# A gated-attention and convolution kernel: g_norm by rows, batch 0 by one cast queue, the norm spread in 32-row pairs, copies and order set anew

## The chip, the cores and the metric

The kernel runs on one core of a Trainium2 chip. The core has TensorE (PE, matrix products into PSUM), VectorE (DVE), ScalarE (ACT), GpSimd (POOL) and SyncE (SP); each runs its own instructions in order, and they wait for one another by semaphores. Loads and stores are issued from the queues of SP, ACT and POOL and run on 16 DMA engines that all queues share; a load issued by POOL can change fp32 to bf16 on its way. The metric is the device time of one execution in microseconds, median of the runs.

## The reference

Eight batches, eight heads, a sequence of 576, a head dimension of 64; the joined model dimension is 512, the inner one 1024.

```python
kv = np.einsum('bhsd,bhse->bhde', k, v)
out = np.einsum('bhsd,bhde->bhse', q, kv)
rms = np.sqrt(np.mean(out * out, axis=-1, keepdims=True) + 1e-06)
x = out / rms * g_norm                       # then (B, S, H * D)
h = np.maximum(x @ w_in, 0.0)
conv_out = sum(conv_w[k] * hp[:, k:k + S, :] for k in range(3))   # hp: h padded by one row at both ends
gate = 1.0 / (1.0 + np.exp(-conv_out))
y = (h * gate) @ w_out
```

The first four lines are the attention without softmax and its norm per head; the rest is a gated network with a convolution over the sequence in each of the 1024 channels.

## The kernel before, in words

Everything is kept transposed: channels on the 128 partitions, the 576 positions of a batch along the free dimension. Two heads (64 + 64 channels) make one of four head pairs t of a batch b. The program is a list of small operations, each a Python function, and the string `ORDER` says in which order they are issued; each engine then runs its own in that order. A token such as `hm.0.3@1` names the operation, its arguments and, behind the @, the buffer that its result takes: rings `a` (three double-bank PSUM buffers) and `b` (two PSUM banks) and several rings in SBUF. A buffer's next user waits for the last reader of the one before.

The operations: `pre` sets constants and issues the first loads; `Lq`, `Lk`, `Lv`, `Li`, `Lo` load q, k, v, w_in and w_out by POOL with a change to bf16; `ca` casts batch 0's first two head pairs, which SP loads as fp32 (L301). `kv` (L313) forms k transposed times v for n head pairs; `kvc` copies the 64x64 blocks into the block-diagonal `kvbd`. `qt`/`qt0` transpose q on PE in 24 or 12 small products, `qc`/`qc0` copy the result to SBUF. `ot` (L377) is the attention product o; `sq` squares it on ACT, `oc` copies it to SBUF.

The norm has two forms. Batch 0 goes head pair by head pair: `on` sums the squares with a block matrix of ones, `nl` takes the reciprocal root, `mu0` multiplies o, g_norm and the root. All other batches go by groups (`NORM`): `ss` sums the squares into 32 partitions for each head pair, `ln` takes the reciprocal root for all in one ACT instruction, `sl` splits it into three bf16 parts on DVE, `sp` (L449) spreads it back to 128 channels by products with the 0/1 matrix `spread`, and `mu` multiplies.

Then `hm` (L466) is one of eight 128-channel blocks of x @ w_in, eight products of 288 columns; `re` the relu copy. `ta` multiplies by the two outer convolution weights, scaled by the middle one (which `ct` transposes and `pc` prepares), `aa` and `ab` add, `sg` is the sigmoid, `mg` the gate product. `om` (L523) is one of nine 128-position blocks of the product with w_out for a pair p of batches, 8 products of 512 columns, in two halves of four for p 0 and 3; `ea` copies the result to SBUF and `st` stores it. `pl`, `ps`, `pn` build `sel`, `spread` and the masks `na`, `nb`.

Of the kernel before, what the change touches and what calls it, by code (L numbers as in the profile page):

```python
# [51 lines left out]
FP32 = mybir.dt.float32  # L52
BF16 = mybir.dt.bfloat16
AX = mybir.ActivationFunctionType
AL = mybir.AluOpType
PSUM = bass.MemoryType.PSUM

NORM = {0: [1], 1: [2, 3], 2: [4, 5], 3: [6, 7]}
CONV = {0: (0, 1), 1: (1, 1), 2: (2, 2), 3: (4, 2), 4: (6, 1), 5: (7, 1)}
# [3 lines left out]
pre@0,0,0,1 ca.q.0 qt0.0@0 qc0.0@0 ca.k.0 ca.v.0 kv.0.0.1@0 kvc.0.0.1.0 kvc.0.0.1.1 ot.0.0@1 sq.0.0@0 on.0@2  # L63
ca.v.1 ca.k.1 ca.q.1 qt0.1@0 kv.0.1.1@1 kvc.0.1.1.1 nl.0@0 Lk.1.0@1 qc0.1 kvc.0.1.1.0 qt0.2@2 ot.0.1@0
kv.0.2.1@0 qc0.2@1 sq.0.1@1 kv.0.3.1@1 on.1@2 kvc.0.2.1.0 mu0.0@0 kvc.0.2.1.1 nl.1@1 ot.0.2@1 kvc.0.3.1.0
Lv.1.0@1 sq.0.2@2 ct@0 on.2@2 nl.2@2 kvc.0.3.1.1 mu0.1 Lq.1.0@1 Li.0 pc Lk.1.2 qt0.3@0 mu0.2 qc0.3 ot.0.3@2
sq.0.3@3 kv.1.0.2@1 on.3@0 kvc.1.0.2.0 pl Lq.1.2 qt.1.0@1 nl.3@3 mu0.3 hm.0.0@0 re.0.0@0 qc.1.0@2 kvc.1.0.2.1
hm.0.1@2 ot.1.0@1 re.0.1 Lv.1.2 qt.1.1@0 Li.1 ta.0.0@0 hm.0.2@2 ps ta.0.1 qc.1.1@3 sq.1.0@4 oc.1.0@4 re.0.2 pn
kv.1.2.2@0 ta.0.2@1 kvc.1.2.2.0 ot.1.1@1 kvc.1.2.2.1 hm.0.3@2 sq.1.1@5 oc.1.1@5 re.0.3 ot.1.2@0 aa.0.0 sq.1.2@6
ot.1.3@1 sq.1.3@7 hm.0.7@2 oc.1.3@6 ss.1@1 oc.1.2@7 ln.0@0 ab.0.0 re.0.7 Lv.2.0@0 Lk.2.0@0 ta.0.3 aa.0.1 sl.0@0  # L70
hm.0.5@1 re.0.5 hm.0.4@0 ab.0.1 re.0.4 sp.1.1@2 sp.1.0@1 sg.0.0 kv.2.0.4@0 sp.1.2@0 mu.1.0 mu.1.1 sp.1.3@1
sg.0.3 hm.0.6@2 mu.1.2 mu.1.3 Lq.2.0@0 qt.2.1@0 sg.0.1 mg.0.0 kvc.2.0.4.0 kvc.2.0.4.1 re.0.6 hm.1.7@1 sg.0.2
re.1.7 Lv.3.0@1 qc.2.1@4 ot.2.3@2 sq.2.3@0 Lk.3.0@1 hm.1.5@0 ot.2.2@1 oc.2.3@0 re.1.5 sq.2.2@1 ta.0.4@0 ta.0.5
oc.2.2@1 aa.0.2 ab.0.2 hm.1.6@2 sg.0.5 sg.0.4 qt.2.0@0 qc.2.0@0 hm.1.2@1 Lq.3.0@1 re.1.6 re.1.2 hm.1.3@0
ot.2.0@2 mg.0.1 kv.3.0.4@1 re.1.3 mg.0.2 ta.0.6@1 oc.2.0@2 sq.2.0@2 ot.2.1@1 kvc.3.0.4.0 oc.2.1@3 sq.2.1@3
hm.1.4@0 ta.0.7 Lo.0 aa.0.3 kvc.3.0.4.1 ta.1.6@0 Lo.1 qt.3.1@2 ab.0.3 sg.0.6 qc.3.1@1 qt.3.0@1 qc.3.0@2 ot.3.3@2
re.1.4 om.0.1.0@0 sg.0.7 mg.0.3 sq.3.3@4 ot.3.1@0 sq.3.1@5 oc.3.1@4 ta.1.4@1 ot.3.0@1 om.0.2.0@1 sq.3.0@6
om.0.2.4 ea.0.2@0 ta.1.7 ot.3.2@0 sq.3.2@7 oc.3.2@5 om.0.1.4 ss.2@1 ea.0.1@1 ta.1.5 ss.3 ln.1@0 oc.3.0@7 aa.1.3
ab.1.3 aa.1.2 Lq.5.0@0 qt.5.0@0 qc.5.0@3 oc.3.3@6 om.0.3.0@0 om.0.3.4 sl.1@1 ea.0.3@2 om.0.0.0@1 ab.1.2 hm.1.1@0
re.1.1 sg.1.5 sg.1.7 sp.2.0@1 sp.3.1@2 mu.2.0@1 om.0.0.4 sg.1.4 mu.3.1 Lv.5.0@0 Lk.5.0@0 sp.2.2@0 mu.2.2  # L80
sp.2.3@1 ea.0.0@3 kv.5.0.4@0 sp.2.1@2 hm.1.0@0 re.1.0 mu.2.3 sp.3.2@1 Lq.6.0@1 mu.2.1 sg.1.6 hm.2.0@2 sp.3.3@0
mu.3.2 Lk.4.0@1 re.2.0@1 kvc.5.0.4.0 mg.1.2 mu.3.3 Lk.6.0@0 ta.1.2@1 kvc.5.0.4.1 hm.2.5@1 re.2.5 sp.3.0@2
Lv.4.0@1 mu.3.0 ta.1.3 aa.1.1 mg.1.3 hm.2.7@0 ab.1.1 re.2.7 ot.5.0@1 sq.5.0@0 ta.1.0@0 hm.2.1@2 oc.5.0@2 re.2.1
hm.3.1@0 re.3.1 sg.1.3 ta.1.1 hm.3.0@1 re.3.0 qt.5.1@2 sg.1.2 qc.5.1@4 hm.2.6@0 re.2.6 aa.1.0 ot.5.3@1 oc.5.3@4
sq.5.3@1 kv.4.0.4@1 ot.5.1@2 oc.5.1@1 sq.5.1@2 hm.3.7@0 kvc.4.0.4.0 mg.1.1 re.3.7 hm.2.3@1 re.2.3 Lq.4.0@0
ab.1.0 ta.2.0@1 hm.3.3@2 sg.1.0 ta.2.1 hm.3.2@0 aa.2.0 sg.1.1 ab.2.0 re.3.2 mg.1.0 re.3.3 kvc.4.0.4.1 hm.2.2@1
# [500 lines left out]
```

## Time and profile before

| what | value |
|---|---|
| runs | 194.63, 195.0, 196.04 us, median 195.0 |
| profiled execution | span 192.5 us from the first to the last instruction |
| PE busy | 171.1 us (89%), 1753 products |
| DVE busy | 148.8 us (77%), 279 instructions |
| ACT busy | 153.5 us (80%), 246 instructions |
| POOL busy | 25.7 us, 39 instructions |
| granted TensorE clock | 1.000 |
| loads by POOL | 15.37 MB as landed, 52.7% of the 16 DMA engines over the span |

Some groups of instructions of the page (mean of one by form): sq 673 ns, oc 662, re 658, ea 605, sigmoid 775 for 576 and 1251 for 1152 elements, table load 1283 (eight of them), all on ACT; mu 810, qc 754, aa, ab and mg 757 for 1152 and 1355 for 2304 elements, a tap product 373 or 540, the two casts of batch 0's k and v 615 to 634, on DVE.

How to read it: busy time is the union of an engine's instructions; those queued behind one another overlap a little, so that the sum of their durations is larger. Idle time of an engine that is not the last to be ready costs nothing. The chain of waits goes back from the last instruction to whatever released each step.

### The profile page before, as it was taken

The numbers are of one execution on the slowest core, as the hardware profiler recorded it, in microseconds if no ns is written. First come the engines' busy times: TensorE is split into PE (matmuls) and PEld (weight loads), VectorE is DVE, ScalarE is ACT, GpSimd is POOL, SyncE is SP. The second block draws the span as 40 slices with busy tenths as digits, with TensorE's granted clock in tenths as the row PEclk, the third lists the DMA queues.
The fourth block names the chain that finished last, engine by engine and source line by source line (L and its number), as shares of the span: only waits on it lengthen the run. The fifth ranks groups of instructions, "written<-read, shape, count | busy, mean of one in ns | idle before, by whom it ended". The sixth has DMA issues, their size and how long they took to land.

```text
span 192.5 us, 4249 instructions
## 1 busy us (share of the span) xinstructions
PE 171.1 (89%) x1753; PEld 106.9 (56%) x1753; DVE 148.8 (77%) x279; ACT 153.5 (80%) x246; POOL 25.7 (13%) x39
## 2 busy tenths in 40 slices
PE   0047799899999999999999999999999999999992
PEld 0024366566745777764658776654477485554440
DVE  3133839897988999999989999999989895977100
ACT  2047648999999899999999999999996869478431
POOL 7435303400430111240000000000000000000000
PEclk9999999999999999999999999999999999999999
DMA  4999999999999997999950000441040010170874
GB/s 135 207 236 204 203 204 203 204 204 206 186 203 204 182 130 118 137 120 188 208 185 5 0 3 0 165 167 54 0 163 3 0 54 3 54 272 0 327 266 170
DMA packets 26517, 26.84 MB, mean 139 GB/s; under 512 B 1388, under 2 KB 21892, under 8 KB 26500
## 3 DMA queue, kind: packets, MB, share of 16 engines
q0 software_dynamic: 19872, 15.37, 52.7%
q1 hardware_dynamic: 6432, 11.21, 16.3%
q8 instruction: 13, 0.21, 0.4%
q10 hardware_dynamic: 196, 0.01, 0.1%
q14 instruction: 4, 0.03, 0.1%
HBM read 32.52 MB, written 9.44 MB: 218 GB/s over the span
## 4 chain that ended last, share of the span: by engine, by line
PE 70%; DVE 11%; ACT 8%; DMA 6%; issue 2%; SPq 1%; ACTq 0%
PE h_ps L471 28%; PE om_ps L528 27%; DMA stg<-in_q_dram 6%; PE qt_ps L343 4%; PE sp_ps L454 4%; PE kv_ps L319 3%; ACT sq L388 2%; PE o_ps L374 2%; DVE taps L493 2%; DVE taps L500 2%; DVE taps L506 2%; DVE taps L494 1%; ACT o L393 1%; ACT h L479 1%; DVE h L518 1%
## 5 line engine op out<-in xcount | busy, mean ns | idle before, releaser
L471 PE MATMUL h_ps<-xT,w_in_sb 128*128 128x288 bf16 x512 | 70.1, 290 | 0.7 <-ACT o L393 0.3
L528 PE MATMUL om_ps<-w_out_sb,h 128*128 128x512 bf16 x288 | 66.7, 379 | 0.1
L471 PEld LDWEIGHTS <-w_in_sb 128*128 128x128 bf16 x512 | 50.0, 99 | 17.1 <-issue 1.5
L479 ACT ACTIVATE h<-h_ps 128x576 bf16<-128x576 f32 x64 | 40.6, 658 | 9.3 <-PE h_ps L471 9.0
L528 PEld LDWEIGHTS <-h 128*128 128x128 bf16 x288 | 27.8, 98 | 30.2 <-issue 0.7
L512 ACT ACTIVATE taps<-taps,cw 128x576 bf16<-128x576 bf16 (+1 forms) x48 | 42.9, 933 | 1.0 <-DVE taps L506 0.9
L534 ACT ACTIVATE row<-om_ps 128x512 f32<-128x512 f32 x36 | 21.8, 605 | 10.7 <-PE om_ps L528 10.4
L518 DVE TENSOR_TENSOR h<-h,taps 128x1152 bf16<-128x1152 bf16 (+1 forms) x24 | 22.7, 953 | 5.7 <-ACT taps L512 5.7
L500 DVE TENSOR_TENSOR taps<-taps 128x1152 bf16<-128x1152 bf16 (+1 forms) x24 | 23.0, 958 | 0.5
L343 PE MATMUL qt_ps<-ident,q_sb 96*64 96x96 bf16 x384 | 12.6, 221 | 12.0 <-ACT q_sb L305 11.9
L506 DVE TENSOR_TENSOR taps<-taps,h 128x1152 bf16<-128x1152 bf16 (+1 forms) x24 | 22.9, 956 | 0.5
L493 DVE TENSOR_SCALAR taps<-h,cw 128x576 bf16<-128x576 bf16 (+1 forms) x48 | 20.8, 434 | 2.5 <-ACT h L479 2.5
L460 DVE SCALAR_TENSOR_TENSOR xT<-o,g_sb,sp_ps 128x576 bf16<-128x576 f32 x28 | 21.2, 810 | 1.8 <-PE sp_ps L454 1.8
L494 DVE TENSOR_SCALAR taps<-h,cw 128x576 bf16<-128x576 bf16 (+1 forms) x48 | 20.3, 423 | 0.0
L343 PEld LDWEIGHTS <-q_sb 96*64 96x64 bf16 x384 | 10.4, 120 | 15.9 <-ACT q_sb L305 12.4
L388 ACT ACTIVATE sq<-o_ps 128x576 bf16<-128x576 f32 x28 | 18.1, 673 | 0.1
L393 ACT ACTIVATE o<-o_ps 128x576 f32<-128x576 f32 x28 | 17.8, 662 | 0.0
L374 PE MATMUL o_ps<-qT,kvbd 128*128 128x512 bf16 x32 | 12.7, 409 | 0.0
L196 ACT ACT_TABLE_LOAD x8 | 10.3, 1283 | 2.8 <-issue 2.6
L368 DVE COPY qT<-qt_ps 128x1152 bf16<-128x1152 bf16 x14 | 10.4, 754 | 1.7 <-PE qt_ps L343 1.4
L454 PE MATMUL sp_ps<-wparts,spread 128*128 128x288 bf16 x56 | 9.9, 287 | 1.0 <-ACT h L479 0.7
L276 POOL DMA_DIRECT2D q_sb<-in_q_dram x8 | 6.0, 748 | 34.5 <-PE qt_ps L343 29.0
(66 smaller groups left out, 100.2 us busy)
## 6 DMA issues: line engine op xcount, KB each, us to landing
out_dram<-row SPq DMA_DIRECT2D x36, 256.0 KB, 2.6
v_sb<-in_v_dram POOLq DMA_DIRECT2D x6, 576.0 KB, 9.4
k_sb<-in_k_dram POOLq DMA_DIRECT2D x6, 576.0 KB, 11.3
q_sb<-in_q_dram POOLq DMA_DIRECT2D x6, 576.0 KB, 9.1
w_in_sb<-in_moe_w_in_dram POOLq DMA_DIRECT2D x2, 512.0 KB, 12.8
w_out_sb<-in_moe_w_out_dram POOLq DMA_DIRECT2D x2, 512.0 KB, 15.6
stg<-in_k_dram SPq DMA_DIRECT2D x2, 288.0 KB, 6.2
stg<-in_v_dram SPq DMA_DIRECT2D x2, 288.0 KB, 7.0
```

What stands on the lines that cost most here:

```text
L343: nc.tensor.transpose(ps[i * D:(i + 1) * D, r * PS:(r + 1) * PS], qkv["q", b][:, 2 * t + i, r * D:(r + 1) * D], ident[:PS, :PS])
L388: nc.scalar.activation(by_r(s), natural(o), AX.Square)
L471: nc.tensor.matmul(ps[:, e, :HS], w_in_sb[:, t, f * P:(f + 1) * P], x[:, t, e * HS:(e + 1) * HS], start=(t == 0), stop=(t == NT - 1))
L479: nc.scalar.activation(T["h", b // 2][:, f, b % 2, :].rearrange("p (e n) -> p e n", e=2), T["hm", b, f][:, :, :HS], AX.Relu)
L493: nc.vector.tensor_scalar_mul(tap[:, 0, f % 2, :n, 8:8 + S], h[:, f], cw[:, f:f + 1])
L494: nc.vector.tensor_scalar_mul(tap[:, 1, f % 2, :n, :S], h[:, f], cw[:, 2 * NF + f:2 * NF + f + 1])
L500: nc.vector.tensor_add(tap[:, 1, :, :n, :S], tap[:, 0, :, :n, 7:7 + S], tap[:, 1, :, :n, 1:1 + S])
L506: nc.vector.tensor_add(y, y, h[:, 2 * j:2 * j + 2])
L512: nc.scalar.activation(y, y, AX.Sigmoid, scale=cw[:, NF + f:NF + f + 1])
L518: nc.vector.tensor_mul(h, h, T["tap", c, j][:, 1, :, :n, :S])
L528: nc.tensor.matmul(T["om", p, m], h[:, f, m * P:(m + 1) * P], w_out_sb[:, f, :], start=(f == 0), stop=(f == NF - 1))
L534: nc.scalar.activation(T["os", p, m], T["om", p, m], AX.Copy)
```

## The change

It has five parts.

1. g_norm is loaded twice as a 256-byte row, side by side in a 25th row of `cw_rows`, and the transpose `ct` of the convolution weights brings it to the partitions too; `g_sb` is a column of that result (`cw`, copied by the new `pg`). The scaled weights get a tile of their own, `cwn`.
2. SP loads only k and v of batch 0's first head pair as fp32. The other ten pieces of batch 0 come by POOL with a change to bf16, two of them issued ahead of `affine_select`, which makes the identity.
3. `sp` uses for each head pair only the 32 rows that hold its part, at its place in the array, and does two head pairs in one operation, their products in turn; `spread` shrinks from 2048 to 512 elements, and a pair takes two `a` buffers at once.
4. Every copy out of PSUM (`kvc`, `qc0`, `qc`, `oc`, `re`, `ea`) can run on DVE or ACT by a digit behind a colon in the order. In the new order DVE takes 9 of 28 oc, 7 of 64 re, 5 of 36 ea, 7 of 24 kvc and 1 of 4 qc0; ACT takes 4 of 14 qc and 17 kvc. An oc on DVE waits for the square of the same o on ACT. `pl` fills `sel` on POOL. A `+n` in the order would add filling products; no token has one.
5. The order is new throughout: batches 4 and 5 are loaded ahead of w_out, and batch 4 is attended ahead of batch 5.

```diff
-pre@0,0,0,1 ca.q.0 qt0.0@0 qc0.0@0 ca.k.0 ca.v.0 kv.0.0.1@0 kvc.0.0.1.0 kvc.0.0.1.1 ot.0.0@1 sq.0.0@0 on.0@2
...
+pre@0,0,0 ca.k.0 ps pi ca.v.0 kv.0.0.1@0 ct@1 Lv.1.0@1 qt0.0.0@0 Lq.1.0@1 Lk.1.0@1 pg kv.0.1.1@1 qt0.0.2@1 Li.0
+Lq.1.2 qt0.0.1@2 pc kvc.0.0.1.0@0 qc0.0.0:1@0 kvc.0.1.1.0:1 kvc.0.0.1.1:1 al.x0@0 qc0.0.2:1@1 al.h1@0 kvc.0.1.1.1
+al.h0@1 ot.0.0@0 al.x1@1 sq.0.0@0 on.0.0@1 nl.0.0@0 kv.0.2.1@0 qc0.0.1:1 kvc.0.2.1.0 kvc.0.2.1.1 ot.0.2@1 sq.0.2@1
...
+ss.3 qc.4.1@3 hm.1.4@2 hm.1.2@1 ln.1@0 ta.1.1 oc.3.0@7 qt.4.0@0 re.1.4 sl.1@0 aa.1.0 re.1.2 Lq.5.0@1 sp.3.0@2,1
+mu.3.0 mu.3.1 qc.4.0:1@4 Lv.5.0@1 Lk.5.0@1 sp.2.1@0,2 mu.2.2 mu.2.3 Lo.0 kv.4.0.4@0 Lo.1 sg.0.4 kvc.4.0.4.0@0
+kvc.4.0.4.1 sp.2.0@1,0 mu.2.1 mu.2.0 sg.0.5 ot.4.1@2 sq.4.1@0 qt.5.0@0 oc.4.1@7 ot.4.2@1 sq.4.2@1 mg.0.2 hm.2.2@2
...
+mg.5.0 st.3.0 re.7.6:1 ta.5.6@0 ta.5.7 sg.5.4 ea.3.3@5 om.2.2.0@0 sg.5.5 aa.5.3 om.2.5.0@1 st.2.0 ab.5.3 ea.2.2@3
+om.3.7.0@0 mg.5.2 ea.2.5@6 st.2.2 sg.5.6 st.3.3 sg.5.7 st.2.6 om.2.1.0@1 st.2.5 mg.5.3 ea.2.1@7 om.3.7.4 ea.3.7@1
+om.3.5.0@1 om.3.8.0@0 om.3.5.4 ea.3.5@3 om.3.8.4 ea.3.8@5 om.3.6.0@1 om.3.4.0@0 om.3.6.4 st.3.7 st.2.1 st.3.5
+om.3.4.4 ea.3.6:1@2 st.3.8 st.3.2 st.3.1 st.3.6 ea.3.4@6 st.3.4
...
-        for t in range(2):
-            for x in "kvq":
-                nc.sync.dma_start(out=T["stg"][:, "kvq".index(x), t], in_=heads(x, 0, 2 * t, 2))
+        for i, x in enumerate("kv"):
+            nc.sync.dma_start(out=T["stg"][:, i], in_=heads(x, 0, 0, 2))
...
-            nc.scalar.dma_start(out=g_sb[i * D:(i + 1) * D, :], in_=g_norm.unsqueeze(1))
+            nc.scalar.dma_start(out=cw_rows[NC:, i * D:(i + 1) * D], in_=g_norm.unsqueeze(0))
         act_table("rs")
+        nc.vector.memset(fill, 1.0)
...
+        for n, (x, t) in enumerate([(x, t) for t in range(NT) for x in "kvq" if t or x == "q"]):
+            if n == 2:
+                nc.gpsimd.affine_select(
+                    out=ident, in_=ident, compare_op=AL.not_equal, fill=1.0,
+                    base=0, pattern=[[-1, P]], channel_multiplier=1)
+            nc.gpsimd.dma_start(out=qkv[x, 0][:, 2 * t:2 * t + 2, :], in_=heads(x, 0, 2 * t, 2))
...
+    def after(ins, other):
+        if ins.engine != other.engine:
+            tc.add_manual_dep(
+                ins, other.name,
+                mybir.DependencyInfo(mybir.DependencyClass.Sync, mybir.DependencyReason.DATA), reason="bank")
+
+    def copy(to, fr, on_act):
+        if on_act:
             nc.scalar.activation(to, fr, AX.Copy)
         else:
             nc.vector.tensor_copy(to, fr)
...
-        nc.scalar.activation(by_r(s), natural(T["ot", b, t][:, :S]), AX.Copy)
+        copy(by_r(s), natural(T["ot", b, t][:, :S]), pick[0] == 0)
+        after(last(), T["sqi", b, t])
...
-    def sp(b, t):
+    def sp(b, u):
         g = NG[b]
         bi = NORM[g].index(b)
-        ps = T["sp", b, t] = ring("a", [P, 2, 512], FP32, name="sp_ps")
+        for t in (2 * u, 2 * u + 1):
+            T["sp", b, t] = ring("a", [P, 2, 512], FP32, name="sp_ps")
         for e in range(2):
-            nc.tensor.matmul(
-                ps[:, e, :HS], spread[:, t * 4 + 2 * bi + e, :, :].rearrange("p i d -> p (i d)"), T["w", g],
-                start=True, stop=True)
+            for t in (2 * u, 2 * u + 1):
+                rows = slice(t * 32, (t + 1) * 32)
+                nc.tensor.matmul(
+                    T["sp", b, t][:, e, :HS], spread[rows, 2 * bi + e, :, :].rearrange("p i d -> p (i d)"),
+                    T["w", g][rows], start=True, stop=True, tile_position=(t * 32, 0))
...
+        if pick[0] == 0:
+            nc.scalar.activation(to, fr, AX.Relu)
+        else:
+            nc.vector.tensor_scalar(to, fr, 0.0, None, op0=AL.max)
```

## The prediction

> **What bounds the kernel now.** I read the page's busy times and slices first, then the table of busy times by stretch, then the chain of waits in order of time, then the timeline of the start. The stretches (columns: stretch, its length, then PE, weight loads, DVE, ACT and POOL busy with instruction counts, clock, DMA share, GB/s):
>
> ```profile
> 5.00:10.00 5.00, 0.00 (x0) 0.00 (x0) 0.71 (x1) 0.59 (x1) 2.40 (x4) 1.00 0.97 215
> 10.00:15.00 5.00, 2.31 (x28) 1.16 (x28) 1.60 (x4) 1.99 (x4) 2.18 (x3) 1.00 1.24 228
> ...
> 30.00:40.00 10.00, 8.75 (x136) 5.81 (x132) 9.15 (x22) 9.51 (x18) 3.80 (x5) 1.00 1.32 204
> 40.00:50.00 10.00, 9.53 (x134) 6.67 (x130) 8.76 (x16) 9.95 (x19) 2.06 (x3) 1.00 1.28 205
> 50.00:60.00 10.00, 9.45 (x171) 5.90 (x170) 9.08 (x21) 9.84 (x19) 1.79 (x3) 1.00 1.28 195
> 60.00:70.00 10.00, 10.00 (x110) 6.72 (x109) 8.77 (x14) 9.37 (x15) 1.54 (x2) 1.00 0.98 159
> 70.00:80.00 10.00, 9.98 (x141) 7.62 (x139) 9.87 (x21) 9.60 (x19) 1.78 (x2) 1.00 0.90 130
> ```
>
> Four stages. Nothing runs on PE until 10.3 us (loads). From 10 to 26 us batch 0 goes through one serial chain per head pair. From 26 to 60 us ACT is full (29.3 of 30 us) and the loads run at 204 GB/s. From 60 us on PE is full to 188.8 us; then a copy and a store end the span. Busy PE overstates its work, so I priced each product from pieces of the chain where PE runs without a gap:
>
> ```profile
> 63.60 0.49 PE sp_ps L454 x4
> 64.09 0.86 PE om_ps L528 x4
> ...
> 66.68 0.98 PE h_ps L471 x8
> ...
> 74.67 0.63 PE qt_ps L343 x24
> 75.30 1.09 PE h_ps L471 x8
> ```
>
> That is 0.1225 us for a spread or h product, 0.216 for an om product, 0.63 for 24 transposes, 0.88 for 48 kv products. Over the program: h 62.7, om 62.2, transposes 10.1, kv 7.0, o and on 8.6, spread 6.9, ss 2.4: 160 us. PE ends at 188.8, so it lost 28.8 us: 20.4 before its first h product (25.9 us less 5.5 us of work issued by then), about 6 between 26 and 60 us, about 2 later. The profiled execution's span is 192.5 us; the median run is 195.0, so 2.5 us lie around the span, and I add them at the end.
>
> **The spread (sp).** Before, 56 products of 128 rows one after another: 56 x 0.1225 = 6.86 us, all on a full PE or just before it becomes full. After, the same 56 work on 32 rows each, in pairs on different rows into different PSUM tiles. If the two of a pair overlap wholly, 28 x 0.1225 = 3.43 us: 3.43 saved. The trace has no products side by side in rows. It has them side by side in columns, the sums of squares:
>
> ```profile
> 35.40 0.43 PE L427 MATMUL ss_ps<-sq,sel 128*32 128x288 bf16 x8
> ```
>
> Eight of 0.286 us each within 0.43 us; in a row they would need 0.98. So bounds are 0 (no overlap) and 3.43; I take overlap, by this nearest row. Against it: the 8 h products behind a block of transposes take 1.09 us, and 0.98 behind a spread, so 0.11 goes where the array changes its shape. The 14 blocks of pairs could pay that once each, 1.5 us, or nothing; I take 0.7. Net -2.7 us.
>
> The Trainium skill, page "TensorE: Matmul & The Clock Gate", section on packing small matmuls, reports 3.07 times for four 32-row products; as an estimate from that, a pair would run some 1.5 times as fast and save 2.4 us. The Trainium skill, "TensorEngine Tiling (Array Packing)", section Tiling Modes, says that a change of tiling mode drains the array, which speaks against pairs strewn between full products; the 0.11 us above agrees in sign.
>
> **The start.** Before, batch 0's first two head pairs come as fp32 by SP, and ACT and DVE cast them; the first transposes wait for q:
>
> ```profile
> 9.41 0.84 ACT L305 ACTIVATE q_sb<-stg 96x768 bf16<-96x768 f32 x1 [5.50 <-DMA stg<-in_q_dram]
> 10.31 0.50 PEld L343 LDWEIGHTS <-q_sb 96*64 96x64 bf16 x12 [10.31 <-ACT q_sb L305]
> ...
> 25.68 0.82 DVE L413 SCALAR_TENSOR_TENSOR xT<-o_ps,g_sb,o 128x576 bf16<-128x576 f32 x1 [1.60 <-ACT o L404]
> ```
>
> k and v of the first pair landed at 4.0 and 5.0 us; the six SP loads alternated with the POOL loads from then on (one of each per 1.8 us). After, SP brings only those two, and ten cast loads of 0.63 to 0.75 us issue time follow on POOL. Between loads of POOL alone, landings 0.72 us apart for 144 KB are 204 GB/s. From about 5 to 6 us for q of pair 0 the seventh load, q of pair 2, lands at about 10.5 (bounds: 9.5, and 12.6, where the third POOL load landed before). PE's new order has the transposes of pairs 2 and 1 ahead of the first o product, so that starts at about 11.2 us, where it was 11.9. Four rounds o, square, on, root, multiply follow, 13.8 us before (11.9 to 25.7). In these the first root stood on ACT behind q's second cast, which waited for its load until 14.57 and ended at 15.3, 1.4 us after the product for it; that wait goes, of which I count 0.8, since the kvc copies now on ACT fall in its place. The last multiply then starts at 11.2 + 13.0 = 24.2 instead of 25.7: -1.5 us, bounds -3 and +1 (q of pair 2 at 12.6). w_in's first half had 885 KB of batch 0 and 885 of batch 1 ahead of it on POOL and landed at 22.8; it now has 1,475 and 885, but four SP loads fewer: not later. ACT's two casts (1.7 us) and two of DVE's (1.2) go, beside waits.
>
> g_norm came as two loads of 64 pieces (landing 5.3 and 6.7 us after issue) and is now two rows transposed with conv_w. ct moves ahead of the first transposes and waits for these rows, at the latest 8.7 us; queued behind it on PE are all of batch 0's products, but the first o product waits past 10 us anyway: nothing, or up to 1.6 us if the loads came early. The two extra issues ahead of affine_select (1.4 us) delay ident to 2.5 us, before the first cast at 4.1. The fill tile costs one memset (0.27 us, row of kvbd's) at the start: the order has no token that asks for fills.
>
> **Copies.** From ACT go 9 oc (0.662), 7 re (0.658), 5 ea (0.605), 1 qc0 (0.648) and 2 casts (0.842): 15.9 us; it gets 4 qc of 1152 elements, at most the sigmoid's 1.25 each, 5.0. ACT falls from 153.5 to about 142.6. DVE gets the 22 copies at ACT's price, 14.2 us (bounds 0.5 and 0.81 each, by its casts from SBUF and its multiply L460), and loses 4 qc (3.0), 2 casts (1.2), about 1.0 of spread, 0.6 of sel (now POOL), 0.5 of small ones: from 148.8 to about 157. Summed durations are 8% above busy time because queued instructions overlap by some 0.09 us; if that overlap were complete, 149. I take 153. So DVE becomes the fuller engine. Adding both orders' instructions by these rows, less the overlap: up to its 35th us of PE work the old order asks 41 us of ACT and 37 of DVE, the new one 40.5 and 43. Where ACT was late in the stretch 26 to 60, DVE is late now: I book 0, with bounds -2.4 (ACT's relief counts fully; the loads allow no more, since k of batch 5 has 11.4 MB ahead on POOL, 56 us at 204 GB/s from a start at 5 to 9, and is due after 37 us of PE work: PE has lost at least 24 us by then, against 26.4 before) and +5 (DVE as below). A new wait: an oc on DVE must follow ACT's square of the same tile; behind it on DVE stand conv taps that ACT's sigmoids wait for. At up to a square's 0.67 us each, nine are 0 to 6 us of idle DVE, inside the bound of +5. pl's nine memsets now stand on POOL ahead of batch 2's loads, whose predecessors are still in flight: 0. The tail: after the last h product 24 om products more than before cover the chain ta, aa, ab, sigmoid, mg (about 11 us, covered by 12.1): 0, or +1.
>
> **Sum.** 192.5 - 2.7 - 1.5 = 188.3 span, + 2.5 = **190.8 us**.
>
> **Rivals.**
> *DVE becomes the bound (slower).* By 25 us DVE has done about 7 us; its last mg has 9 half om blocks (7.8), a copy and store (3.7) behind it. Span = 25 + 146/u + 11.5, u its use until then. u = 0.96 gives the forecast's 188.6, 0.92 195.2, so 197.7 us; each per cent is 1.6 us. For it: 90% between 30 and 60 us. Against: 97% from 70 to 130. It decides below 0.94. Chance 0.22, times 194 to 200.
> *Slots.* A pair holds two of three PSUM slots until its multiplies. At batches 2 and 3 the order sets sp.3.0, sp.2.1, kv.4, sp.2.0, ot.4.1, qt.5.0 in a row with no om block between: an add of 0.7 and five multiplies of 0.78 are 4.6 us on DVE before qt.5.0 gets its slot, beside 1.9 us of PE work: 2.7 lost, 193.5. For it: there the old order has om blocks, and w_out now comes later. Against: the same stretch is bound by DVE anyway. Chance 0.11.
> *The pairs bring nothing.* Draining into and out of each of 14 blocks at 0.11 costs 3.1 and eats the 3.43; or the rows don't overlap, which is the case where the change doesn't do what it says: 193.2 to 194. Chance 0.10. The first would be the rule of the Trainium skill, "TensorEngine Tiling (Array Packing)", section Tiling Modes.
> *More.* ACT's relief counts fully and DVE keeps up: 190.8 - 2.4 - some of the start: 187. Chance 0.15.
>
> **Numbers.** The forecast's own case has 0.42, between 188.8 and 193. About 1% (1.95 us) is what a measurement tells from no change. Faster by over 1% (below 193.05): forecast, "more" and 0.01 of the slots: 0.58. Within: 0.08 of slots, 0.10 of pairs, 0.04 of DVE's: 0.22. Slower (above 196.95): 0.18 of DVE's, and 0.02 where slots and DVE add up: 0.20. Range 185.5 to 197.5: below lies the far end of "more", above the worse half of DVE's.
>
> **What would show it.** Pairs: 8 spread products within 0.5 us, an h block behind them at 0.98 to 1.1. Start: first o product near 11.2, first h product near 24.5. Copies: DVE over 95% from 30 to 130 us, ACT below 95%. It would be wrong if PE shows waits for DVE between 60 and 130 us, or if q of pair 2 lands after 12.6.

## The result, and the profile after

The changed kernel takes 198.23 us (median of 13 runs, 196.1 to 199.69) and the kernel before, beside it, 194.63 (193.74 to 196.04): 1.0145 times as long, 95% interval 1.0116 to 1.0174. The ratio leaves disturbed runs out, so it is a little below that of the medians. The prediction was 190.8 us with a range of 185.5 to 197.5: the kernel is some 1.5% slower where faster was forecast, and outside the range. The profiled execution took 196.1 us, with a span of 194.3, and is the shortest of the 13.

The table of busy times by stretch, of the changed kernel (columns as before: stretch, length, PE, weight loads, DVE, ACT, POOL, clock, DMA share, GB/s):

```profile
5.00:10.00 5.00, 1.71 (x37) 1.55 (x37) 3.13 (x17) 0.87 (x2) 5.00 (x9) 1.00 1.30 195
10.00:15.00 5.00, 2.86 (x40) 1.67 (x40) 0.80 (x1) 3.07 (x7) 4.66 (x14) 1.00 1.31 199
30.00:40.00 10.00, 7.38 (x124) 4.89 (x122) 9.89 (x18) 9.65 (x16) 1.78 (x3) 1.00 1.32 204
40.00:50.00 10.00, 9.42 (x177) 6.75 (x172) 9.18 (x19) 8.81 (x16) 3.69 (x5) 1.00 1.20 177
50.00:60.00 10.00, 7.71 (x147) 4.62 (x145) 9.32 (x18) 9.88 (x15) 2.53 (x4) 1.00 1.31 203
60.00:70.00 10.00, 9.61 (x153) 6.50 (x146) 8.78 (x16) 8.80 (x17) 4.54 (x6) 0.83 1.28 205
70.00:80.00 10.00, 9.97 (x79) 5.46 (x78) 9.06 (x19) 9.67 (x16) 0.11 (x1) 1.00 1.32 204
```

The first two rows are better than before, and three are worse. PE works from 6.2 us on, where it had nothing until 10.3. But from 30 to 40 us it is busy for 7.38 us instead of 8.75, from 50 to 60 for 7.71 instead of 9.45, and from 60 to 70 its clock is 0.83 on average where it was 1.00. Busy time does not tell how much work is done at half a clock, so I priced every product as the prediction did and subtracted: "lost" is the time so far less the work of the products started so far, so it holds waits and slow clock together. The prices are 0.1225 us for one product of h or spread, 0.216 of om, 0.63 for 24 transposes, 0.88 for 48 of kv, 0.24 for an o or on, and 0.043 for one of ss. The last two rows are experiments told below.

| lost by PE, us | by 26 us | by 50 | by 65 |
|---|---|---|---|
| before | 20.8 | 25.8 | 26.7 |
| changed | 18.4 | 23.7 | 29.0 |
| before with the new start alone | 17.7 | 21.9 | 22.2 |
| before with start, rows and pairs | 18.4 | 22.6 | 23.1 |

At 26 us the changed kernel leads by 2.4 us, at 50 by 2.1, at 65 it is 2.3 behind. From 70 us on PE is nearly full in both. So the change wins at the start and loses 5.3 us between 50 and 65, where the kernel before loses 0.9.

What PE does there, in the timeline of the changed kernel (start, duration, engine, line, operation, count, and in brackets the idle time before it and what ended it):

```profile
57.50 0.42 PE L497 MATMUL sp_ps<-wparts,spread 32*128 32x288 bf16 x4 [0.49 <-DVE wparts L486]
58.35 0.28 PE L497 MATMUL sp_ps<-wparts,spread 32*128 32x288 bf16 x1 [0.43 <-ACT qT L328]
58.90 0.40 PE L497 MATMUL sp_ps<-wparts,spread 32*128 32x288 bf16 x3 [0.27 <-DVE xT L503]
59.23 0.95 PE L342 MATMUL kv_ps<-v_sb,k_sb 96*64 96x64 bf16 x48
60.11 0.64 PE L497 MATMUL sp_ps<-wparts,spread 32*128 32x288 bf16 x4
61.10 0.23 PE L403 MATMUL o_ps<-qT,kvbd 128*128 128x64 bf16 x1 [0.35 <-ACT kvbd L328]
61.15 0.61 PE L404 MATMUL o_ps<-qT,kvbd 128*128 128x512 bf16 x1
```

This is the row of operations sp.3.0, sp.2.1, kv.4, sp.2.0, ot.4.1 that the prediction's second rival names. Four of the seven lines wait, two for DVE and two for ACT, and there is no om block among them; the first om product of the changed kernel starts at 70.8 us. The big product at 61.15 takes 0.61 us, where the same one takes 0.38 at 50.2 and at 64.9 us. The reason stands in the table of busy times taken microsecond by microsecond (columns as above):

```profile
57.00:58.00 1.00, 0.43 (x6) 0.11 (x5) 1.00 (x2) 1.00 (x2) 0.00 (x0) 1.00 1.33 207
58.00:59.00 1.00, 0.38 (x3) 0.18 (x3) 1.00 (x3) 0.98 (x2) 0.00 (x0) 1.00 1.31 209
59.00:60.00 1.00, 1.00 (x51) 0.78 (x48) 1.00 (x2) 0.99 (x2) 0.00 (x0) 1.00 1.32 198
60.00:61.00 1.00, 0.74 (x16) 0.25 (x8) 1.00 (x3) 0.99 (x3) 0.00 (x0) 1.00 1.32 205
61.00:62.00 1.00, 0.87 (x9) 0.44 (x11) 1.00 (x3) 0.95 (x3) 0.83 (x2) 0.52 1.29 201
62.00:63.00 1.00, 1.00 (x26) 0.88 (x23) 1.00 (x2) 1.00 (x2) 1.00 (x2) 0.50 1.28 208
63.00:64.00 1.00, 1.00 (x5) 0.53 (x5) 1.00 (x4) 0.46 (x2) 0.50 (x1) 0.50 1.23 205
64.00:65.00 1.00, 1.00 (x9) 0.69 (x6) 1.00 (x3) 0.79 (x2) 0.00 (x0) 0.77 1.26 208
```

After one microsecond of 0.43 and one of 0.38 busy, the granted clock halves at 61.0 us and comes back at 64.5. In between PE looks full and does half its work. DVE and ACT are full beside it, much as the prediction had it; its forecast did not expect that PE would have nothing of its own to do meanwhile.

The start, in the timelines of PE and DVE:

```profile
10.25 1.17 PE L364 MATMUL qt_ps<-ident,q_sb 96*64 96x96 bf16 x24 [2.31 <-DMA q_sb<-in_q_dram]
11.35 0.24 PE L403 MATMUL o_ps<-qT,kvbd 128*128 128x64 bf16 x1
11.40 0.61 PE L404 MATMUL o_ps<-qT,kvbd 128*128 128x512 bf16 x1
...
23.46 0.82 DVE L453 SCALAR_TENSOR_TENSOR xT<-o_ps,cw,o 128x576 bf16<-128x576 f32 x1 [1.59 <-ACT o L438]
```

q of pair 2 is there at 10.25 us (forecast 10.5), the first o product starts at 11.35 (11.2), the last multiply of batch 0 at 23.46 (24.2; before, 25.68).

The spread, in the chain of waits of the changed kernel:

```profile
82.70 0.35 PE sp_ps L497 x4
83.05 0.88 PE kv_ps L342 x48
...
122.84 1.73 PE om_ps L573 x8
124.57 0.35 PE sp_ps L497 x4
124.92 1.83 PE om_ps L573 x8
```

Four spread products take 0.35 us instead of 0.49. Eight om products take 1.73 behind an h block and 1.83 behind a spread block. So of the 0.14 won, 0.10 goes behind it; the 48 kv products take their 0.88 as before.

### The profile page after: what moved, and what is told of

It reads as the page before. It is cut to its first block, busy times and chain, and to the rows that moved or that the text cites. A ratio compares the mean times of both kernels' runs of the same rounds, so it can differ in the third digit from the quotient of the medians.

```text
span 194.3 us, 4238 instructions
## 1 busy us (share of the span) xinstructions
PE 171.9 (88%) x1753; PEld 103.4 (53%) x1753; DVE 157.5 (81%) x282; ACT 146.4 (75%) x227; POOL 29.1 (15%) x52
## 4 chain that ended last, share of the span: by engine, by line
PE 76%; ACT 11%; DVE 5%; DMA 2%; POOL 2%; issue 1%; POOLq 0%; ACTq 0%
PE om_ps L573 33%; PE h_ps L515 29%; PE qt_ps L364 5%; PE o_ps L404 3%; PE kv_ps L342 2%; DMA q_sb<-in_q_dram 2%; ACT h L524 2%; PE sp_ps L497 2%; ACT qT L328 1%; ACT L201 1%; ACT sq L419 1%; ACT o L438 1%; ACT kvbd L328 1%; DVE o L330 1%; PE o_ps L403 1%
## 5 line engine op out<-in xcount | busy, mean ns | idle before, releaser
L557 ACT ACTIVATE taps<-taps,cwn 128x576 bf16<-128x576 bf16 (+1 forms) x48 | 42.9, 935 | 2.2 <-DVE taps L551 2.0
L524 ACT ACTIVATE h<-h_ps 128x576 bf16<-128x576 f32 x57 | 35.5, 654 | 7.7 <-PE h_ps L515 6.2
L328 ACT ACTIVATE row<-om_ps 128x512 f32<-128x512 f32 x31 | 18.2, 597 | 15.9 <-PE om_ps L573 14.2
L503 DVE SCALAR_TENSOR_TENSOR xT<-o,cw,sp_ps 128x576 bf16<-128x576 f32 x28 | 21.4, 809 | 1.6 <-PE sp_ps L497 1.6
L539 DVE TENSOR_SCALAR taps<-h,cwn 128x576 bf16<-128x576 bf16 (+1 forms) x48 | 20.4, 426 | 0.0
L538 DVE TENSOR_SCALAR taps<-h,cwn 128x576 bf16<-128x576 bf16 (+1 forms) x48 | 19.9, 415 | 0.2
L342 PE MATMUL kv_ps<-v_sb,k_sb 96*64 96x64 bf16 x384 | 9.3, 206 | 6.2 <-DVE v_sb L315 6.2
L404 PE MATMUL o_ps<-qT,kvbd 128*128 128x512 bf16 x32 | 13.4, 423 | 0.0
L342 PEld LDWEIGHTS <-k_sb 96*64 96x64 bf16 x384 | 8.1, 120 | 8.9 <-DVE k_sb L315 5.0
L328 ACT ACTIVATE o<-o_ps 128x576 f32<-128x576 f32 x19 | 12.5, 667 | 0.0
L201 ACT ACT_TABLE_LOAD x8 | 10.3, 1283 | 2.1 <-issue 2.0
L453 DVE SCALAR_TENSOR_TENSOR xT<-o_ps,cw,o 128x576 bf16<-128x576 f32 x4 | 3.3, 817 | 10.3 <-ACT o L438 10.3
```

The source lines that it names most:

```text
L328: nc.scalar.activation(to, fr, AX.Copy)
L342: nc.tensor.matmul(ps[i * D:(i + 1) * D, t - t0, :], k_sb[:, 2 * t + i, r * D:(r + 1) * D], v_sb[:, 2 * t + i, r * D:(r + 1) * D], start=( ...
L503: nc.vector.scalar_tensor_tensor(x_tile(b)[:, t, :].rearrange("p (e n) -> p e n", e=2), T["o32", b, t].rearrange("p (e n) -> p e n", e=2), ...
L524: nc.scalar.activation(to, fr, AX.Relu)
L539: nc.vector.tensor_scalar_mul(tap[:, 1, f % 2, :n, :S], h[:, f], cwn[:, 2, f:f + 1])
L557: nc.scalar.activation(y, y, AX.Sigmoid, scale=cwn[:, 1, f:f + 1])
```

## The experiments

Times are medians; ratios are to the kernel before in the same comparison (194.67 to 195.01 us), with 95% intervals. Lines of the order are cut to the tokens around a change.

**The start alone.** The kernel before with the changed kernel's loads of batch 0; the order is kept but for the casts that are gone.

```diff
-        for t in range(2):
-            for x in "kvq":
-                nc.sync.dma_start(out=T["stg"][:, "kvq".index(x), t], in_=heads(x, 0, 2 * t, 2))
+        for i, x in enumerate("kv"):
+            nc.sync.dma_start(out=T["stg"][:, i], in_=heads(x, 0, 0, 2))
...
-        for t in range(2, NT):
-            for x in "kvq":
-                nc.gpsimd.dma_start(out=qkv[x, 0][:, 2 * t:2 * t + 2, :], in_=heads(x, 0, 2 * t, 2))
+        for n, (x, t) in enumerate([(x, t) for t in range(NT) for x in "kvq" if t or x == "q"]):
...
-pre@0,0,0,1 ca.q.0 qt0.0@0 qc0.0@0 ca.k.0 ca.v.0
+pre@0,0,0,1 qt0.0@0 qc0.0@0 ca.k.0 ca.v.0
...
-ca.v.1 ca.k.1 ca.q.1 qt0.1@0
+qt0.1@0
```

> The kernel before with the new start alone: SP brings k and v of the first head pair, POOL the other ten pieces of batch 0 in the new order, two ahead of the identity. Theory 'order' (the changed kernel wins 2.4 us at its start and gives them back, and more, in a stretch at 50 to 65 us that its order leaves without om blocks): first h product at 22 to 24.5 us instead of 25.9, and most of it kept to the end, 192.5 to 193.5 us against 194.6, ratio 0.989 to 0.995. Rival 'loads and ACT' (the stretch from 26 to 60 us is bound by ACT and the loads anyway and swallows an earlier start): ratio 0.998 to 1.002.

Measured: 190.73 us, ratio 0.9782 (0.9733 to 0.983). The start is worth 4.2 us by the ratio, twice what was expected, and this kernel is faster than both. In the old order the first o product starts at 9.18 us (before 11.87; changed kernel 11.35, since that one has two more blocks of transposes ahead of it and waits 2.31 us for their q), the first h product at 21.77 (before 25.90), PE has lost 3.1 us less by 26 us, and 3.9 less by 50. Its om blocks stand in the stretch that starves in the changed kernel; its PE timeline:

```profile
51.05 1.89 PE L527 MATMUL om_ps<-w_out_sb,h 128*128 128x512 bf16 x8
52.78 0.19 PE L372 MATMUL o_ps<-qT,kvbd 128*128 128x64 bf16 x1
52.81 0.38 PE L373 MATMUL o_ps<-qT,kvbd 128*128 128x512 bf16 x1
53.03 1.03 PE L527 MATMUL om_ps<-w_out_sb,h 128*128 128x512 bf16 x4
53.98 0.67 PE L426 MATMUL ss_ps<-sq,sel 128*32 128x288 bf16 x16
54.71 0.70 PE L342 MATMUL qt_ps<-ident,q_sb 96*64 96x96 bf16 x24
55.35 2.76 PE L527 MATMUL om_ps<-w_out_sb,h 128*128 128x512 bf16 x12
```

Between the o products of batch 3, the sums of squares and the transposes of batch 5 stand om blocks, and no line has a wait in brackets. om needs no result of ACT or DVE that is not long there, and asks of them one copy of 0.6 us per 1.73 us of PE work.

**g_norm as rows.** The same kernel with the change's first part: a 25th row, the transpose moved ahead of the second pair's kv products.

```diff
-            nc.scalar.dma_start(out=g_sb[i * D:(i + 1) * D, :], in_=g_norm.unsqueeze(1))
+            nc.scalar.dma_start(out=cw_rows[3 * NF:, i * D:(i + 1) * D], in_=g_norm.unsqueeze(0))
...
-qt0.1@0 kv.0.1.1@1
+qt0.1@0 ct@1 kv.0.1.1@1
```

> The kernel before with the new start loads (190.7 us) and the change's first part added: g_norm as two 256-byte rows beside conv_w's, brought to the partitions by the same transpose, which moves ahead of the second head pair's kv products. The prediction booked this at nothing, or up to 1.6 us if the product that waits for the rows came early. Theory: within 0.5 us of 190.7, since the rows land before 8.7 us and the products behind the transpose wait for q and k until then. Rival: 192 us, PE waiting for cw_rows ahead of the second pair's kv.

Measured: 191.03 us, ratio 0.9795 (0.9742 to 0.9848). Nothing, as booked.

**Pairs alone, and the change without them.** First the kernel before with 32-row products, nine pairs where its order has two spread operations next to one another on PE, ten single ones elsewhere. Then the changed kernel with products of 128 rows again.

```diff
-                ps[:, e, :HS], spread[:, t * 4 + 2 * bi + e, :, :].rearrange("p i d -> p (i d)"), T["w", g],
-                start=True, stop=True)
+            T["sp", b, t][:, e, :HS], spread[rows, t * 4 + 2 * bi + e, :, :].rearrange("p i d -> p (i d)"),
+            T["w", g][rows], start=True, stop=True, tile_position=(t * 32, 0))
```

> The kernel before with the spread's products on 32 rows; where two spread operations follow each other on PE (9 places) they are one, with their four products in turn; the other ten stay single. Theory 'pairs bring nothing' (four products take 0.35 us instead of 0.49, and the om or h block behind them 0.11 more): ratio 0.998 to 1.004, the blocks behind at 0.97 or 1.09 instead of 0.86 or 0.98. Rival, the forecast's term: 9 x 0.245 saved = 2.2 us, ratio 0.988.

> The changed kernel with the spread's products on all 128 rows again, same order, same two buffers at a time. Theory 'pairs bring nothing': within 0.8 us of the changed kernel, ratio to before 1.010 to 1.018; if the 32-row products count little as work for the clock, the drop at 61 us goes and it is 1 to 2 us faster than the changed kernel (1.003 to 1.010). Rival, the forecast's term: 3.4 us slower than the changed kernel, ratio 1.030.

Measured: pairs alone 195.61 us, ratio 1.0045 (1.0015 to 1.0075); the change without pairs 197.45, ratio 1.0128 (1.0077 to 1.0179), against 1.0145 with them. They win nothing. The chain of waits gives the account, here for a single block of two products, first in the kernel before, then with 32 rows:

```profile
67.66 0.24 PE sp_ps L454 x2
67.90 0.98 PE h_ps L471 x8
```

```profile
67.88 0.35 PE sp_ps L458 x2
68.22 1.09 PE h_ps L483 x8
```

On 32 rows two products take 0.35 us, as long as the four of a pair above. So the two products of a pair that use different rows do overlap wholly, and a block on 32 rows costs 0.10 us more itself and makes the block behind it 0.10 longer. A pair block then saves 0.03 us between full products, and 0.14 ahead of kv products; a single block costs 0.1 to 0.2. Added up over the blocks of the chain that is +1.2 us, and +0.9 was measured (0.3 to 1.5 by the interval). Without pairs the clock of the changed kernel stays at 1.00 from 56 to 66 us, though PE is busy for only 0.51, 0.73 and 0.70 us in three of them running; PE still loses 4.9 us from 50 to 65.

**The shares alone.** The kernel before in its old order with each copy on the engine that the changed kernel uses for it (a square that stood behind its oc goes ahead of it), and the reverse: the changed kernel, its order kept token for token, with every copy back on its old engine.

```diff
-        nc.scalar.activation(by_r(s), natural(T["ot", b, t][:, :S]), AX.Copy)
+        copy(by_r(s), natural(T["ot", b, t][:, :S]), "oc", b, t)
+        if ("sqi", b, t) in T:
+            after(last(), T["sqi", b, t])
```

```diff
-re.0.0:1 pl re.0.2
+re.0.0 pl re.0.2
...
-mu.3.0 mu.3.1 qc.4.0:1@4
+mu.3.0 mu.3.1 qc.4.0@4
```

> The kernel before, in its order, with the new shares of the copies: the same oc, re, ea, kvc, qc0 and qc on DVE or ACT as in the changed kernel, each oc on DVE behind its square. Theory 'order': the shares by themselves cost little, ratio 0.995 to 1.008. Rival 'DVE is overloaded' (a copy of 576 fp32 takes 0.75 us on DVE, not 0.66, and DVE had 1 to 3% left from 70 to 130 us): 2 to 5 us slower, ratio 1.010 to 1.025.

> The changed kernel, its order kept token for token, with every copy out of PSUM back on the engine that it had before (kvc of batch 0 and qc on DVE, qc0, the other kvc, oc, re and ea on ACT). Theory (the order without om blocks in the stretch from 48 to 65 us is at fault, whoever copies): within 2 us of the changed kernel, 196 to 200 us. Rival (DVE's new share is at fault): 2 to 5 us faster, 193 to 196. That shares set for one order are poison in another (as the old order with the new shares showed, 225.7 us) would be the third case: over 203 us.

Measured: 225.71 us, ratio 1.157 (1.15 to 1.164), for new shares in the old order, and 207.97, ratio 1.068 (1.0628 to 1.0731), for old shares in the new one. The first misses what either theory gave, the second is its third case. Where the first goes, from the waits of its DVE (who waited for whom: us in total, times, longest):

```profile
DVE o L320 <- ACT sq L407: 9.3, 7, 3.7
DVE kvbd L320 <- ACT kvbd L318: 9.0, 2, 6.1
```

Its DVE is not too full; it stands behind copies that wait for ACT's squares, an addition that the prediction put "inside the bound of +5". The reverse waits too, from PE's waits between 40 and 80 us:

```profile
PE sp_ps L496 <- DVE qT L329: 2.4, 1, 2.4
```

So shares and order are one plan, and neither run measures what the shares are worth alone. The second says one thing of DVE, in its busy times (columns as above):

```profile
50.00:65.00 15.00, 9.10 (x156) 5.96 (x155) 9.13 (x17) 13.44 (x22) 3.38 (x5) 0.93 1.31 204
```

With its old copies DVE is busy for 9.13 of these 15 us, PE loses 7.1 of them, and the kernel is some 10 us slower than with the new shares. So taking load off DVE does not cure the changed order; ACT, which gets the copies, is close to full.

**om blocks as cover.** The new start with the old order and old shares, but pair 0's first four om blocks (6.9 us of PE work) moved behind the transposes of batch 4. In the profile the first om product then starts at 80.5 us; in the changed kernel that is 70.8.

```diff
-re.1.4 om.0.1.0@0 sg.0.7 mg.0.3 sq.3.3@4 ot.3.1@0 sq.3.1@5 oc.3.1@4 ta.1.4@1 ot.3.0@1 om.0.2.0@1 sq.3.0@6
-om.0.2.4 ea.0.2@0 ta.1.7 ot.3.2@0 sq.3.2@7 oc.3.2@5 om.0.1.4 ss.2@1 ea.0.1@1 ta.1.5 ss.3 ln.1@0 oc.3.0@7
+re.1.4 sg.0.7 mg.0.3 sq.3.3@4 ot.3.1@0 sq.3.1@5 oc.3.1@4 ta.1.4@1 ot.3.0@1 sq.3.0@6
+ta.1.7 ot.3.2@0 sq.3.2@7 oc.3.2@5 ss.2@1 ta.1.5 ss.3 ln.1@0 oc.3.0@7
...
-qt.4.1@2 om.0.5.0@0
+qt.4.1@2 om.0.1.0@0 om.0.2.0@1 om.0.1.4 ea.0.1@1 om.0.2.4 ea.0.2@0 om.0.3.0@0 om.0.0.0@1 om.0.3.4 ea.0.3@2 om.0.0.4
+ea.0.0@3 om.0.5.0@0
```

> The kernel before with the new start (190.7 us) and nothing else of the change, but pair 0's first four om blocks (and their ea copies) moved from where batches 2 and 3 are normed to behind the transposes of batch 4, about where the changed kernel has them; copies, loads and spread stay as before. Theory (the changed order loses its time because no om blocks cover the norm of batches 2 and 3 and the o products of batch 5): the stretch from 48 to 65 us starves as in the changed kernel, 3 to 5 us are lost by 70 us and not won back, 193.5 to 196 us, PE lost by 70 us 23 to 25 us (19.5 without the move). Rival (DVE's larger share of the copies is what starves that stretch): within 1 us of 190.7.

Measured: 197.84 us, ratio 1.0156 (1.0103 to 1.021). The move costs 7.1 us, more than expected, and brings the kernel to the changed one's time. Its busy times (columns as above):

```profile
50.00:55.00 5.00, 2.32 (x41) 1.46 (x42) 4.15 (x11) 4.84 (x9) 1.53 (x2) 0.93 1.31 204
55.00:60.00 5.00, 4.15 (x45) 2.46 (x39) 4.73 (x9) 3.72 (x6) 0.00 (x0) 0.50 1.32 204
60.00:65.00 5.00, 4.92 (x75) 3.39 (x74) 4.64 (x7) 4.88 (x7) 1.55 (x2) 0.88 1.20 180
```

PE has 2.32 of 5 us to do, and then works at half its clock for 7 us. (A few o products lack a record here, at most 1 us of it.) ACT and DVE, with the old shares, are nearly as full as in the changed kernel: 13.4 and 13.5 of these 15 us, there 14.1 and 14.3. So the stretch starves without DVE's larger share.

**What of it is the clock.** The same kernel with two products of 512 columns that nobody reads in each of the eight places where a half om block stood.

```diff
+    @op
+    def unb(n):
+        ps = ring("b", [P, 512], FP32, name="unb_ps")
+        for _ in range(n):
+            nc.tensor.matmul(ps, fill[:, :P], fill, start=True, stop=True)
...
-re.1.4 sg.0.7 mg.0.3 sq.3.3@4
+re.1.4 unb.2@0 sg.0.7 mg.0.3 sq.3.3@4
```

> The kernel with pair 0's early om blocks moved behind the transposes of batch 4 (197.8 us; 190.7 without the move), with two products of 512 columns that nobody reads in each of the eight places where a half om block stood (3.5 us at full clock). They do none of the work. Theory: some 2 to 2.5 of the 7.1 us are the clock, which stood at 0.50 from 55 to 60 us and 0.93 and 0.88 beside it, and the rest is work that PE could have done and did not; the clock then stays at 1.00 and the time is 195 to 196.5. Rival (all of it is clock): 191 to 193. Rival (the clock costs nothing, since ACT and DVE are waited for anyway): 197.3 to 199.

Measured: 196.66 us (195.98 to 197.08, where the one without them has 197.81 to 198.24), ratio 1.0106 (1.0078 to 1.0135). Its busy times in the same stretches:

```profile
50.00:55.00 5.00, 4.27 (x54) 2.06 (x54) 4.29 (x10) 4.97 (x8) 0.62 (x1) 1.00 1.31 202
55.00:60.00 5.00, 4.45 (x61) 2.57 (x62) 4.89 (x10) 4.38 (x7) 0.00 (x0) 1.00 1.32 204
60.00:65.00 5.00, 4.96 (x60) 3.86 (x54) 4.95 (x9) 4.67 (x9) 1.55 (x2) 1.00 1.31 199
```

The clock stays at 1.00, and 1.2 us come back (the runs of the two kernels do not overlap, the intervals of their ratios do); the time is just above what the theory gave. So of the 7.1 us about 1.2 come back with the clock, half of what I expected. The fills take 3.5 us of PE time themselves, so the clock's own cost may be larger; the rest, up to 5.9 us, is work that PE could have done then and has to do later.

**Fills in the changed kernel.**

```diff
-sp.3.0@2,1
+unb.2@0 sp.3.0@2,1 unb.2@1
...
-kv.4.0.4@0
+kv.4.0.4@0 unb.2@1
...
-ot.4.1@2
+ot.4.1+1@2
```

> The changed kernel with seven products of 512 columns that nobody reads put into its stretch of little work from 57 to 61 us (two ahead of the first spread block of batches 2 and 3, two behind it, two behind batch 4's kv, one ahead of its first o product). Theory of the clock (the granted clock halves at 61 us because PE had little to do in the 4 us before): the clock stays at 1.00 from 61 to 65 us, and the kernel is 0.8 to 2 us faster than the changed one, 196.2 to 197.4. Rival (the drop has another cause, or the time that it takes would be waited for anyway): the clock drops all the same, or it does not and the time stays within 0.5 us of the changed kernel's.

Measured: 196.95 us (196.08 to 198.62), ratio 1.0122 (1.0049 to 1.0195). From 56 to 66 us the clock is now 1.00 in every microsecond. The time is 1.3 us lower, but the intervals overlap and it is not resolved. In the profiled execution, one of 198.62 us, the clock halved elsewhere, from 41 to 44 us, where the changed kernel's own profile kept 1.00: where the drop falls is not fixed from one execution to the next. The times go with it: the two executions with a mean clock of 0.991 took 197.72 and 198.62 us, the two with 1.000 took 196.08 and 196.18. The changed kernel without fills has 0.991 in six of the ten executions that its ratio counts (median 196.8 us) and 0.969 to 0.983 in the other four (198.7).

**om blocks back into the changed kernel.** Two om blocks of pair 0 moved into the starved stretch, w_out loaded ahead of batch 5, and what the blocks need brought ahead of the norm.

```diff
-kvc.3.0.4.1 sg.0.6 Lv.4.0@0
+kvc.3.0.4.1 sg.0.6 sg.0.5 sg.0.4 Lv.4.0@0
...
-mg.0.3
+mg.0.3 mg.0.2
...
-Lq.5.0@1 sp.3.0@2,1
+Lo.0 Lo.1 Lq.5.0@1 sp.3.0@2,1 om.0.3.0@1 om.0.3.4
...
-sp.2.0@1,0
+sp.2.0@1,0 om.0.1.0@1 om.0.1.4
```

> The changed kernel with two om blocks of pair 0 (four halves, 3.5 us of PE work) moved from 70.8 us into its starved stretch, one behind the first spread block of batches 2 and 3 and one behind batch 2's last; for them w_out is loaded ahead of batch 5 instead of behind it, and the two sigmoids and the gate product that they need come before the norm's root. Copies, pairs and all other order stay. Theory (the loss is om blocks missing as cover): PE busy from 55 to 65 us rises from 8.43 to about 10 us, no halved clock there, and 2 to 4 us are won, 194 to 196.5 us. Rival (DVE and ACT, both over 95% busy there, set the pace whatever PE does meanwhile): within 1 us of the changed kernel, 197 to 199.5. Third case: batch 5, loaded later, is late, and the time is over 199.5.

Measured: 204.5 us, ratio 1.0501 (1.0475 to 1.0528). A miss, in the direction of the third case but for another reason. From 55 to 65 us PE is busy for 7.99 us, where 10 were expected, and the clock halves there from 57.6 to 61.0. The busy times of the stretch behind the moved blocks (columns as above):

```profile
65.00:70.00 5.00, 4.02 (x78) 2.35 (x80) 3.59 (x5) 0.83 (x3) 2.30 (x3) 1.00 1.32 204
```

ACT, nearly full in the changed kernel, is busy for 0.83 of 5 us. Why, from the timelines of PE and ACT:

```profile
67.69 1.89 PE L572 MATMUL om_ps<-w_out_sb,h 128*128 128x512 bf16 x7 [0.93 <-DVE row L329]
69.42 0.19 PE L402 MATMUL o_ps<-qT,kvbd 128*128 128x64 bf16 x1
...
69.92 0.65 ACT L418 ACTIVATE sq<-o_ps 128x576 bf16<-128x576 f32 x1 [2.77 <-PE o_ps L403]
```

The second om block takes the PSUM bank of the first, whose copy stands on DVE behind two multiplies; PE waits 0.93 us for it and works 1.8 us on the block. Batch 4's first o product is queued behind that, and ACT, whose next piece of work is its square, waits 2.77 us. I had put the cover ahead of a product that feeds a full engine. Besides, the two sigmoids that I brought forward stand on ACT ahead of the copy that batch 3's last o product waits for, 1.96 us instead of 0.62. So a cure of the changed order was tried once and failed on where the blocks were put; it stays open what that order would take with om in a better place.

**All parts but order and shares.** The start, the rows and the spread by 32-row products (nine pairs and ten single ones), in the old order with the old shares; the edits are those above.

> The kernel before with three parts of the change together: the new start loads, g_norm by rows, and the spread by 32-row products (nine pairs, ten single ones, as its own order allows); its copy shares and the rest of its order kept. Theory (the new order, with the shares that belong to it, is all that makes the changed kernel slow, and pairs bring nothing): 191.0 with the start and the rows, plus 0.9 as the pairs cost alone, so 191 to 192.3 us; the changed kernel's remaining 6 to 7 us are then order and shares. Rival (the parts spoil one another, for example pairs that hold two PSUM slots in a kernel that reaches its full PE earlier): 193 to 196.

Measured: 191.19 us, ratio 0.981 (0.9757 to 0.9864). All that is left between this and the changed kernel is the new order with its shares: 1.0145 less 0.981 is 3.35% of 194.7, or 6.5 us. (By the account of the pairs above it is rather more, since ten spread blocks are single here and none is there.)

**One share by itself.** The start alone, with the four kvc copies of batch 1 on DVE.

```diff
-        if b == 0:
+        if b in (0, 1):
             nc.vector.tensor_copy(to, fr)
```

> The kernel before with the new start loads (190.7 us) and only the four kvc copies of batch 1, 64x128 each, moved from ACT to DVE, which is 58 to 69% busy at 20 to 30 us where they stand; ACT is full from 30 us on and these four copies of 0.27 us stand in the chain of waits at 24.4 and 27.6 to 28.0 us. Theory (a copy moved off the full engine where the other one is idle wins what it took): 0.3 to 0.9 us faster, 189.8 to 190.4. Rival (in-order DVE reaches them late, behind conv taps that wait for ACT, as in the old order with all the new shares): 191 to 193.

Measured: 191.64 us, ratio 0.9828 (0.9772 to 0.9883), against 0.9782. Not faster, and within the rival's range; the two intervals overlap. Four copies out of the chain of waits win nothing that shows.

## Why the prediction was wrong, step by step

*The start* (-1.5) was right in mechanism and too small: the landings and the first o product came within 0.25 us of what was worked out, the last multiply 0.7 earlier. In the changed kernel it is 2.4 us by 26 us; in the old order it is 3.1 by then and 4.2 in the end. That order begins the first pair's chain 2.2 us earlier still, since it waits for no q of pair 2. The prediction had the two extra blocks of transposes in view and did not ask what they cost. Some of the 4.2 may be the clock of the first 29 us, as told in the last section.

*The spread* (-2.7) was wrong: the rival "the pairs bring nothing" held, and in the way that it was worked out. The full overlap that the term took from the sums of squares is there: four products in pairs take no longer than two. What was mis-sized is the 0.7 us for 14 changes of shape. The range for it ended at 0.11 us once per block; the lines show 0.10 in the block and 0.10 behind it. That leaves 0.03 us for a block between full products and 0.14 for one beside kv products. Seven of the 14 blocks are of each kind, so at most some 1.2 us is left of the 2.7, an estimate from these rows, and the runs show none of it (197.45 us without pairs, 198.23 with). The Trainium skill, "TensorEngine Tiling (Array Packing)", section Tiling Modes, says that a change of mode drains the array: the lines agree, and the runs put 0.10 us on each change.

*The copies and the order* (booked 0, bounds -2.4 and +5) is the step that failed. Its sentence was "Where ACT was late in the stretch 26 to 60, DVE is late now: I book 0". It counted what the two engines do in the stretch and not what PE has to do while they do it. The totals were good: DVE is busy for 157.5 us (forecast 157), ACT for 146.4 (142.6). (The row that it read as "full (29.3 of 30 us)" is 30 to 60 us; from 26 to 30 ACT is busy for 1.5 of 4.) Where 0 was booked, order and shares together cost 6.5 us. The order loads batches 4 and 5 ahead of w_out, so that no om block can stand beside the norm of batches 2 and 3 and the o products of batch 4, and there, from 50 to 65 us, PE loses 4.4 us more than before. That missing om blocks can cost this much is shown in the old order, where taking them out cost 7.1 us. For the changed order it is argued from the trace: the one cure that was tried there failed, and how the 6.5 us divide between order and shares stays open.

*The rivals.* "Slots" named the place, the row of operations and the cause ("there the old order has om blocks, and w_out now comes later"), and was set aside because "the same stretch is bound by DVE anyway". That reasoning is the error: when DVE and ACT are the bound, PE time in that stretch is free, and work put there is won. It priced the loss at 2.7; it is 4.4 more than before in the profile, since the waits begin at 50 us, with the o products of batch 3, and the clock falls. "DVE becomes the bound" gave 194 to 200 and would fit the time, but not the traces: PE waits for DVE nowhere between 60 and 130 us, and from 50 to 62 us its waits are 1.0 us for DVE and 1.6 for ACT; old shares in the new order are slower, and old shares without the cover lose the same.

*The signs it named.* Eight spread products within 0.5 us: no, 0.70. First h product near 24.5: at 22.44, waiting at 24.33 for the last multiply. DVE over 95% and ACT below it from 30 to 130 us: 93.5 and 93.4%. The two signs of being wrong (PE waiting for DVE behind 60 us, q landing late) did not come. They could not have caught this: the waits for DVE lie ahead of 60 us, and a PE without work shows up as short waits for many engines (0.49, 0.43, 0.27 and 0.35 us above), not as one long one.

## What to carry to other kernels

Where two engines are full and the third is not, list the work that needs only the third, and keep it for that stretch; a new order is to be read for what it takes away there, not only for what each engine has to do. Products that need a late weight (here w_out) are such work, so the weight's place in the load queue decides. It belongs where PE would wait, behind the products that feed the full engines and not ahead of them. A table of busy times per microsecond with the granted clock beside it shows both the hole and what it costs afterwards, and one move of the suspected cover, in the kernel where it still works, is a cleaner test than a repair of the one where it does not.

## What the runs showed of the hardware

The granted clock halved after a stretch in which PE was never idle for more than 0.5 us: 0.43, 0.38, 1.00 and 0.74 busy, with products of 32 rows or 64 columns, then 3.4 us at 0.5. With 128-row products in the same places, 0.51, 0.73, 0.70 busy, it stayed at 1.00, and that kernel's four executions have mean clocks of 0.998 to 1.000, where the changed kernel's thirteen have 0.969 to 0.991. Busy time alone does not decide: in the same profile PE was busy for 1.90 us of the 3.42 from 33.73 us and kept its clock, and for 2.43 of the 3.42 from 57.62 and lost it. What counts as work for the clock stays open.

The Trainium skill, "TensorE: Matmul & The Clock Gate", section "What's actually happening", has the clock halve after an idle window of some 3.4 us in a window that runs freely. The grid agrees: in every trace of this case the time between two changes of the clock is a whole multiple of 3.41 us (in the changed kernel 37.55, 3.41 and 129.71 us). Idle, however, PE was not, and thin work was enough here.

At the start the clock column does not show the slow clock. It reads 1.00 there, but the o product at 11.40 us takes 0.61 us, as at half clock. In every trace that product takes 0.61 us ahead of the first record of the clock, which comes at 21.6 to 31.0 us, and 0.38 behind it unless a halved clock is on record. The first record comes at 28.8 us in the profile of the kernel before and at 21.6 to 27.1 in those with the new start, so some of what the new start wins may be clock; no run separates the two.

In these copies DVE's time goes with the bytes and ACT's with the elements. Copies out of PSUM, from the groups of instructions of the changed kernel (names, shapes, count, busy us and mean ns):

```profile
L330 DVE COPY qT<-qt_ps 128x1152 bf16<-128x1152 bf16 x10 | 7.5, 751 | 1.2 <-PE qt_ps L364 1.2
L330 DVE COPY o<-o_ps 128x576 f32<-128x576 f32 x9 | 6.8, 751 | 1.5 <-ACT sq L419 1.4
L328 ACT ACTIVATE o<-o_ps 128x576 f32<-128x576 f32 x19 | 12.5, 667 | 0.0
L328 ACT ACTIVATE qT<-qt_ps 128x1152 bf16<-128x1152 bf16 x4 | 4.4, 1136 | 0.0
```

1152 bf16 elements take DVE as long as 576 of fp32; ACT takes 1136 against 667 ns. The change gave ACT four of the former and DVE nine of the latter, each to the engine that is slower at it.
